# A second down product in two more gated chunks as seven smaller products, in the last chunk's order

## The chip, the cores and the metric

The kernel runs on one core of a Trainium2 chip. The metric is the device time of one execution in microseconds (us); lower is better. Three runs of the kernel before took 1439.04, 1439.17 and 1439.54 us.

## The reference

Four layers work on x, 2048 rows of 1024 numbers: linear attention (A), a gated block (B), A and B again with the same weights. Only B's down product changes here.

```python
def _B_ref(x, W_gate, W_up, W_down):        # D = 1024, F = 3584
    gate = jnp.einsum("bsd,df->bsf", x, W_gate)
    up = jnp.einsum("bsd,df->bsf", x, W_up)
    gate = gate * (gate > 0)
    h = gate * up
    return jnp.einsum("bsf,fd->bsd", h, W_down)
...
x = x + _A_ref(_layernorm(x), A_wqkv, A_wo)
x = x + _B_ref(_layernorm(x), B_W_gate, B_W_up, B_W_down)
x = x + _A_ref(_layernorm(x), A_wqkv, A_wo)
x = x + _B_ref(_layernorm(x), B_W_gate, B_W_up, B_W_down)
```

## The kernel before

A gated layer (l is 1 or 3) is done in two chunks (c is 0 or 1) of 1024 rows. In each chunk the loop over `u` makes the hidden values h in 14 units of 256 columns (`glu`), and then `down` multiplies h by W_down and adds the result to x. In layer 3 the added rows are the output: `onto` writes them to a tile `xo` (line 1437), which a DMA sends out (line 1438).

Every large product is done by a scheme for two by two blocks that needs seven block products where the plain rule needs eight. In `down` these are called 11, 21, T1, T2, 22, T3 and T4: 11, 21 and 22 use blocks of W_down as they are, the T products use sums of blocks that were made once, in layer 1, and kept in DRAM (`td`). The left side is made of blocks of h (`raw`) or of their sums e1 and e2. A result block is two by two such block results: `first` and `second` are the two groups of 512 rows, and 0 and 1 the two halves of the 1024 columns. 11 goes to first 0 and, as a start (`seed`, a ScalarE copy), to the banks Y that T2, T3 and, where T4 is not divided, T4 add to.

There are two ways to do one of the seven. `product` does it plainly: two halves of the weights (896 KB each), four banks of 128 rows by 512 columns, 56 matmuls (line 1417). `deep` divides it once more by the same scheme: seven products of 14 matmuls with 256 columns each, 98 matmuls (line 1470). For that the weights' block is prepared beforehand: `make_dd` loads it into two slots (`load_dd`), VectorE forms four sums (`sums_dd`, line 1051), and seven blocks go to DRAM (`dd`, stores at line 1042). `deep` then loads them as four entries, three of 896 KB and one of 448 KB (`load_deep`, line 1023). The left side is divided by `inner`, 16 additions of blocks on VectorE (line 1444), spread over the products that come before; within `deep`, ScalarE makes two copies (line 1479), VectorE one sum of banks (line 1495) and the additions to x (line 1430, or 1437 for output).

Before the change, T1 and 22 are divided in every chunk, T4 in all but the first, and 21 in the last chunk alone. The last chunk has an order of its own (the branch at line 1569): 11, T2, T1, T3, 21, 22, T4. The others run 11, 21, T1, T2, 22, T3, T4.

What sets the order of work around it:

- The weights come through a ring of five entries in the order of a list (`plan_B`). When an entry's use begins, `free_before` asks for the loads of the four that follow it in the list (line 1023 or 996 in `down`, lines 1172 and 1176 for the gate and up weights of a unit). The loads are issued by SP, in the order of its queue.
- All large tiles, among them the ring's entries, h (seven), e1 and e2 (two each), the two of `load_dd`, and the next chunk's normalized rows and their sums (`sums_x`, lines 1246 to 1249), share 16 slots. A tile waits until a slot is free.
- `later.at(n, f)` puts a piece of work n ticks later; `product` ticks eight times, `deep` seven times, a unit of `glu` about fourteen. So layer norms of the rows that come next, the preparation of blocks and transfers are spread over the products.
- From this program order a planner sets each engine's queue, and it lets work that is ready go ahead of work that waits.

At the head of layer 1's second chunk (units 0 to 2) VectorE also takes early row statistics for the next layer (`ln_early`), and blocks of the attention weights are loaded, summed and stored (`wq`, `tq`).

Of the kernel before, what the change touches and what calls it, by code (L numbers as in the profile page):

```python
# [92 lines left out]
class _Net:  # L93
# [906 lines left out]
    DEEP = ("T1", "22", "T4", "21")  # L1000

    def is_deep(self, l, c, p):
        return p in {(1, 0): ("T1", "22"), (3, 1): self.DEEP}.get((l, c), self.DEEP[:3])

    def order_d(self, l, c):
        if (l, c) == (3, 1):
            return "11", "T2", "T1", "T3", "21", "22", "T4"
        return "11", "21", "T1", "T2", "22", "T3", "T4"

# [642 lines left out]
    def layer_B(self, l, final):  # L1652
        ring = self.ring

        def behind(it, fn):
            with self.tc.issue_after(it.ins):
                fn()

        for c in range(2):
            hT = []  # L1660
            first = l == 1 and c == 0
            wd = {}
            for u in range(self.U):
                if u % 2 == 0:
                    hT.append(self.slot(f"h{l}_{c}_{u // 2}", dtype=F16))
                ring.load_to(ring.index((l, c, "g", u)) + 5)
                if first:
                    if u + 1 < self.U:
                        for n, w in enumerate("gu"):
                            self.later.at((4 if u else 9) + 4 * n, lambda u=u, w=w: behind(  # L1670
                                self.last_put if u else self.last_z,
                                lambda: self.make_gu(ring.get((l, c, w, u + 1)), w, u + 1)))
                    if u == 3:
                        for d in (self.U - 4, self.U - 2):
                            wd[d] = self.load_d(d)
                        self.make_dd("22", 18)
                    if u in (4, 5, 6):
                        for i, n in enumerate(range(3 * (u - 4), min(3 * (u - 3), 8))):
                            self.later.at(2 + 4 * i, lambda d=self.U - 4 + n // 4 * 2, n=n % 4: behind(
                                self.last_put, lambda: self.sums_d(wd[d], d, (n,))))  # L1680
                    if u == 7:
                        self.make_dd("T1", 1)
                if not final and c == 1:
                    if u in (0, 3):
                        self.load_w("qk"[u // 3])
                    if u in (1, 2, 4, 5):
                        for n in range(2):
                            self.later.at(4 + 5 * n, lambda w="qk"[u // 4], n=2 * (u % 3 - 1) + n: behind(
                                self.last_put, lambda: self.sums_w(w, n)))
                self.plan_inner(l, c, u, hT)  # L1690
                if u % 2 == 0 and u:
                    self.later.at(7, lambda h=hT[-2]: self.behind(self.last_put, self.third_sum, (h,)))
                if (l, c, u) in ((1, 1, 6), (3, 0, 5)):
                    self.make_dd("T4" if l == 1 else "21", 1)
                if c == 0 and u == 1:
                    for n, turn in enumerate(self.turns):
                        self.later.at(1 + n, turn)
                if c == 0 and u in (1, 2):
                    self.later.at(6, lambda u=u: behind(self.last_put, self.pairs[u - 1]))
                self.glu(l, c, u, hT)  # L1700
                if c == 0 and u == 2:
                    self.pairs[2]()
                if c == 0 and u == (self.U - 1 if first else 0):
                    after = self.last_put.ins
                if c == 1 and u == 6:
                    held = self.last_put.ins
            if c == 0:
                self.ln_chunk(l, 1, 20, 3, 3, after)
            elif not final:
                self.ln_later(l + 1, 0, 24, 3, 4, held)  # L1710
                self.ln_later(l + 1, 1, 36, 3, 4, held)
            for n in range(2 if (l, c) in ((1, 1), (3, 0)) else 0):
                self.later.at(2 + n, lambda t=n + (c == 0) * self.NS: self.bring_back(t))
            self.down(l, c, hT, final)
# [58 lines left out]
```

## Time and profile before

| | |
|---|---|
| runs, median (lowest to highest) | 1439.17 us (1439.04 to 1439.54) |
| profiled execution, first to last instruction | 1437.3 us; its own time beyond that is not listed |
| TensorE matmuls | 1429.1 us busy, 7706 |
| VectorE | 1035.7 us busy, 1991 instructions |
| ScalarE | 622.2 us busy, 1137 instructions |
| GpSimd | 309.0 us busy, 220 instructions |
| DMA | 331.31 MB, mean 231 GB/s |
| `down` of layer 1, second chunk | 648.0 to 728.7 us |
| `down` of layer 3, first chunk | 1108.2 to 1188.8 us |
| `down` of layer 3, last chunk | 1354.2 us to the end |

Times are counted from the first instruction. Engines are named PE (TensorE matmuls), PEld (TensorE weight loads), DVE (VectorE), ACT (ScalarE), POOL (GpSimd) and SP (the queue that issues most DMAs); L1470 is line 1470 of the kernel. In a row `out<-in` are the tiles written and read, xcount is the number of instructions, then come the busy time, the mean duration of one in ns, and the engine's idle time before them with what ended it. A matmul's duration includes the filling of the array, so the distance from one to the next is shorter than its duration.

### The profile page before, as it was taken

Reading aid. Unit: us, or ns where it says so; the run is one execution under the profiler, and the core shown is the slowest. Engines: PE = TensorE matmul, PEld = TensorE weight load, DVE = VectorE, ACT = ScalarE, POOL = GpSimd, SP = SyncE. Lnnn points to the kernel's source line nnn. Section 1 sums busy time; section 2 is a strip of 40 time slices with the busy share of each in tenths; the row PEclk is TensorE's granted clock in tenths of the full one; section 3 lists DMA queues with packets and bytes.
Section 4 is the critical chain, followed back from the end, with each engine's and each line's share of the span. In section 5 each row is a group of like instructions: output and inputs, shape, how many; then the busy total and the mean of one; then the engine's idle time right before and its main releaser. Section 6 shows DMA issues by size and latency. Waiting matters only on the chain.

```text
span 1437.3 us, 21281 instructions
## 1 busy us (share of the span) xinstructions
PE 1429.1 (99%) x7706; PEld 735.6 (51%) x7706; DVE 1035.7 (72%) x1991; ACT 622.2 (43%) x1137; POOL 309.0 (21%) x220
## 2 busy tenths in 40 slices
PE   9999999999999999999999999999999999999998
PEld 4444444444456444545654444445554565555457
DVE  7978698778685676558778885865766764666785
ACT  7873564233425234332058725733443434444201
POOL 1453860010100010110031577410111011111102
PEclk9999999999999999999999999999999999999999
DMA  9950787999659999866983118998878799775565
GB/s 284 243 162 8 171 208 201 292 317 292 204 190 308 350 355 334 278 216 209 292 281 100 60 22 248 278 281 261 263 226 297 225 305 281 215 203 170 175 238 180
DMA packets 360889, 331.31 MB, mean 231 GB/s; under 512 B 109840, under 2 KB 321296, under 8 KB 359760
## 3 DMA queue, kind: packets, MB, share of 16 engines
q1 hardware_dynamic: 352208, 307.15, 71.7%
q10 hardware_dynamic: 7136, 18.88, 3.5%
q0 software_dynamic: 1440, 3.93, 0.8%
q8 instruction: 60, 0.98, 0.3%
q14 instruction: 45, 0.37, 0.1%
HBM read 243.66 MB, written 61.60 MB: 212 GB/s over the span
## 4 chain that ended last, share of the span: by engine, by line
PE 94%; DVE 4%; ACT 1%; issue 0%; DMA 0%; DVEq 0%; ACTq 0%
PE ps L506 11%; PE yu L1275 9%; PE yg L1275 9%; PE dy L1417 8%; PE xg L1275 7%; PE xu L1275 6%; PE dx L1417 6%; PE i L1128 5%; PE ps L789 4%; PE zu L1275 3%; PE zg L1275 3%; PE my L588 3%; PE dyT L1470 2%; PE mv L588 2%; PE mx L588 2%; PE vu L1275 2%
## 5 line engine op out<-in xcount | busy, mean ns | idle before, releaser
L1275 PEld LDWEIGHTS <-w 128*128 128x128 f16 (+1 forms) x2768 | 270.6, 98 | 295.0 <-issue 3.7
L506 PE MATMUL ps<-w,xnT 128*128 128x512 bf16 x768 | 169.9, 379 | 0.7 <-DVE xnT L356 0.3
L1355 POOL TENSOR_TENSOR h<-m5u,m5g 128x512 f16<-128x512 f32 x28 | 37.1, 1326 | 423.4 <-DVE m5u L1351 253.4
L506 PEld LDWEIGHTS <-xnT 128*128 128x128 bf16 x768 | 74.3, 98 | 90.5 <-issue 1.8
L1275 PE MATMUL xg<-xnT,w 128*128 128x512 f16 x448 | 115.3, 379 | 0.0
L1275 PE MATMUL xu<-xnT,w 128*128 128x512 f16 x448 | 115.0, 379 | 0.0
L1417 PEld LDWEIGHTS <-h 128*128 128x128 f16 x672 | 65.7, 98 | 78.3
L1470 PEld LDWEIGHTS <-h 128*128 128x128 f16 x966 | 94.5, 98 | 12.3
L1355 POOL TENSOR_TENSOR h<-c22u,c22g 128x512 f16<-128x512 f32 x28 | 35.6, 1271 | 289.9 <-DVE c22u L1351 247.6
L1275 PE MATMUL yu<-s,w 128*128 128x512 f16 x376 | 96.5, 379 | 0.5 <-DVE zu L1331 0.5
L1275 PE MATMUL yg<-s,w 128*128 128x512 f16 x376 | 96.8, 379 | 0.0
L449 ACT ACTIVATE e<-e,eps 128x512 f32<-128x512 f32 x128 | 91.0, 720 | 3.2
L736 POOL TENSOR_TENSOR kvc<-pq,kvc 128x1024 f32<-128x1024 bf16 x32 | 78.6, 2455 | 53.1 <-DVE den L741 32.7
L1417 PE MATMUL dx<-w,h 128*128 128x512 bf16 x392 | 85.3, 379 | 0.0
L789 PE MATMUL ps<-T,pqT 128*128 128x512 bf16 x384 | 83.6, 379 | 0.0
L1302 DVE TENSOR_TENSOR h<-yu,r 128x512 f16<-128x512 f32 x56 | 38.6, 690 | 55.8 <-PE yu L1275 55.8
L1299 ACT ACTIVATE r<-yg 128x512 f32<-128x512 f32 x56 | 33.4, 597 | 101.5 <-PE yg L1275 101.5
L527 POOL TENSOR_TENSOR kvc<-kvc,slab 128x512 f32<-128x512 f32 x46 | 57.2, 1248 | 76.0 <-DVE slab L452 72.7
L448 ACT ACTIVATE e<-ps 128x512 f32<-128x512 f32 x92 | 54.2, 589 | 28.6 <-PE ps L506 28.1
L1128 PEld LDWEIGHTS <-x 128*128 128x128 f16 x504 | 49.2, 98 | 33.5 <-issue 1.9
L1299 ACT ACTIVATE r<-zg 128x512 f32<-128x512 f32 x56 | 32.8, 586 | 70.8 <-PE zg L1275 70.8
L748 POOL TENSOR_TENSOR pq<-pq,den 128x1024 bf16<-128x1024 bf16 x32 | 61.2, 1914 | 6.8 <-DVE den L743 6.8
(274 smaller groups left out, 2597.0 us busy)
## 6 DMA issues: line engine op xcount, KB each, us to landing
w<-in_B_W_gate_dram SPq DMA_DIRECT2D x56, 512.0 KB, 6.1
w<-in_B_W_up_dram SPq DMA_DIRECT2D x56, 512.0 KB, 5.4
w<-ddT SPq DMA_DIRECT2D x21, 896.0 KB, 6.3
w<-td SPq DMA_DIRECT2D x18, 896.0 KB, 4.8
x<-away SPq DMA_DIRECT2D x30, 512.0 KB, 7.5
w<-dd SPq DMA_DIRECT2D x15, 896.0 KB, 5.9
w<-in_B_W_down_dram SPq DMA_DIRECT2D x14, 896.0 KB, 6.1
away<-x SPq DMA_DIRECT2D x24, 512.0 KB, 6.8
```

What stands on the lines that cost most here:

```text
L449: self.last_exp = nc.scalar.activation(out=e, in_=e, func=ACT.Exp, scale=-1.0, bias=self.eps6[:, 0:1])
L506: nc.tensor.matmul(by_row(ps), lhsT=self.xnT[l, l_q][:, kt, j * P:(j + 1) * P], rhs=w[:, kt, :].rearrange("p (b i d) -> p i b d", i=R, d=H ...
L588: nc.tensor.matmul(banks[j], lhsT=A(i)[:, j * P:(j + 1) * P], rhs=B(i), start=start and i == 0, stop=i == NS - 1, skip_group_check=True)
L736: nc.gpsimd.tensor_tensor(out=prod, in0=pq_of[sc, j], in1=zrow, op=ALU.mult)
L748: nc.gpsimd.tensor_tensor(out=heads(pq), in0=heads(pq), in1=den[:, :].unsqueeze(2).to_broadcast([P, D // HD, HD]), op=ALU.mult)
L789: nc.tensor.matmul(ps, lhsT=pqT[sc][:, g, j * P:(j + 1) * P], rhs=T[g // 4][:, g % 4, n2 * NW:(n2 + 1) * NW], start=(g == 0), stop=(g == G ...
L1128: nc.tensor.matmul(b[:, w, :], lhsT=B[p][:, w, k, :], rhs=A[p][:, k, :], start=start and w == 0 and k == 0, stop=k == 1, skip_group_check= ...
L1275: nc.tensor.matmul(ps, lhsT=W[w][m][:, k, :], rhs=A[m][:, k, :], start=start and k == 0, stop=k == 3, skip_group_check=True)
L1299: self.last_relu = nc.scalar.activation(out=out, in_=ps, func=ACT.Relu)
L1355: nc.gpsimd.tensor_tensor(out=h[:, 3, :], in0=V["u"], in1=V["g"], op=ALU.mult)
L1417: nc.tensor.matmul(banks[j], lhsT=A(k)[:, j * P:(j + 1) * P], rhs=w[:, i, :], start=start and k == 0, stop=k == self.U - 1, skip_group_che ...
L1470: nc.tensor.matmul(out, lhsT=A[i // 2][:, i % 2, j * P:(j + 1) * P], rhs=B[m][:, i, :], start=start and i == 0 and j == 0, stop=i == NK - ...
```

## The change

Product 21 is divided in layer 1's second chunk and layer 3's first as well, and both take the last chunk's order of products. The prepared blocks of 21 are therefore needed earlier: `make_dd("21")` moves from unit 5 of layer 3's first chunk to unit 0 of layer 1's second. Layer 1's first chunk stays as it is.

```diff
     def is_deep(self, l, c, p):
-        return p in {(1, 0): ("T1", "22"), (3, 1): self.DEEP}.get((l, c), self.DEEP[:3])
+        return p in (("T1", "22") if (l, c) == (1, 0) else self.DEEP)
 
     def order_d(self, l, c):
-        if (l, c) == (3, 1):
+        if self.is_deep(l, c, "21"):
             return "11", "T2", "T1", "T3", "21", "22", "T4"
         return "11", "21", "T1", "T2", "22", "T3", "T4"
...
-                if (l, c, u) in ((1, 1, 6), (3, 0, 5)):
-                    self.make_dd("T4" if l == 1 else "21", 1)
+                if (l, c, u) in ((1, 1, 0), (1, 1, 6)):
+                    self.make_dd("T4" if u else "21", 1)
```

In `down` the branch at line 1569 asks `is_deep(l, c, "21")`, so it now serves three chunks; in it 11 is also added to x by itself (`eleven_done`, four more additions), and 21 is added by five additions from its banks instead of four.

## The prediction

> **What bounds the kernel now.** I read the page's busy times and chain first, then the waits of TensorE alone between 420 and 1430 us, which hold both chunks that change.
>
> ```profile
> span 1437.3 us, 21281 instructions
> PE 1429.1 (99%) x7706; PEld 735.6 (51%) x7706; DVE 1035.7 (72%) x1991; ACT 622.2 (43%) x1137; POOL 309.0 (21%) x220
> PE 94%; DVE 4%; ACT 1%; issue 0%; DMA 0%; DVEq 0%; ACTq 0%
> ```
>
> ```profile
> PE qx L690 <- DVE qy L681: 0.3, 1, 0.3
> PE ps L506 <- DVE pq L452: 0.2, 1, 0.2
> PE qv L690 <- DVE qm L681: 0.2, 1, 0.2
> PE fold L772 <- DVE kvc L640: 0.2, 1, 0.2
> ```
>
> The reader is to see that TensorE carries 94% of the chain and that the listed waits in 1010 us add up to 0.9 us, with no DMA among them. So the time falls by what TensorE no longer has to do, and by hardly anything else; but every wait that the change creates is paid in full.
>
> The third view is the chain in order of time (start, us, engine, tile, line, count).
>
> ```profile
> 648.00 24.17 PE dx L1417 x112
> 672.17 1.53 PE dxT L1470 x14
> 683.39 11.87 PE dy L1417 x55
> ...
> 1132.37 1.53 PE dxT L1470 x14
> 1143.41 11.87 PE dy L1417 x55
> ...
> 1366.31 12.09 PE dy L1417 x56
> 1401.31 1.53 PE dx L1470 x14
> 1412.01 1.53 PE dx L1470 x14
> ```
>
> The first five rows are the two chunks that change, layer 1's second and layer 3's first: 112 large matmuls are products 11 and 21, then come T1's small ones from 672.17 and 1132.37, then T2. The last three are the last chunk: T2 as 56 large matmuls, then the starts of the divided 21 and 22.
>
> **The change part by part.** *Matmuls.* A plain product is 56 matmuls in 12.09 us (the 1366.31 row). The divided 21 runs from 1401.31 to 1412.01, 10.70 us for 98 matmuls of half the columns. That replaces 12.09 us once in each of two chunks: 2 x 1.39 = 2.78 us saved, all of it on the path. Reordering the other six products changes no count.
>
> *Work on VectorE and ScalarE in the two down stages.*
>
> ```profile
> L1430 DVE TENSOR_TENSOR x<-x,dx 128x512 f32<-128x512 f32 x4 | 2.6, 676 | 0.0
> L1444 DVE TENSOR_TENSOR h<-e 128x512 f16<-128x512 f16 x6 | 2.3, 415 | 0.0
> L1479 ACT ACTIVATE dy<-dx 128x512 f32<-128x512 f32 x2 | 1.2, 582 | 29.5 <-PE dx L1470 29.5
> ```
>
> Product 11 now adds its four banks to x, product 21 adds five instead of four: 5 adds x 0.676 us more. The division brings 16 block sums, four of them on half-size blocks (at most 16 x 0.415 = 6.6 us), and one bank sum of an addition's size (0.7 us): at most 3.4 + 6.6 + 0.7 = 10.7 us of VectorE per chunk. ScalarE gets two copies, 1.2 us.
>
> ```profile
> 672.20:683.20 11.00, 10.85 (x99) 9.49 (x98) 11.00 (x24) 6.97 (x14) 0.00 (x0) 1.00 0.84 262
> 683.20:695.10 11.90, 11.90 (x58) 5.41 (x57) 9.01 (x17) 0.00 (x0) 0.00 (x0) 1.00 1.07 295
> 695.10:705.90 10.80, 10.80 (x99) 9.58 (x98) 8.28 (x21) 1.18 (x2) 0.00 (x0) 1.00 1.07 357
> 717.90:728.60 10.70, 10.70 (x100) 9.59 (x99) 5.36 (x9) 1.18 (x2) 0.00 (x0) 1.00 1.02 330
> 1143.20:1177.90 34.70, 34.70 (x211) 20.47 (x210) 22.20 (x55) 17.05 (x33) 4.29 (x7) 1.00 1.08 293
> 1401.20:1422.60 21.40, 21.40 (x198) 19.18 (x197) 14.87 (x35) 2.36 (x4) 5.42 (x9) 1.00 0.78 266
> ```
>
> The columns are the stretch, its length, then busy us and counts of PE, PEld, DVE, ACT and POOL, the granted clock, the DMA share and GB/s. In layer 1's second chunk VectorE is full during T1 (11.00 of 11.00), and T1 there lasts from 672.17 to 683.39, 11.22 us, against 11.04 between the matching rows at 1132.37 and 1143.41. Row statistics of the next layer sit there now, because product 21 completes half of the rows early; in the new order those halves are complete only after 21, so I expect them to move to the last product, where VectorE has 5.3 us free (5.36 of 10.70). Bounds of this step: a gain of 0.18 us, if T1 loses its delay, and a loss of 10.7 us less the idle VectorE time behind T1 (2.9 + 2.5 + 5.3 = 10.7 us in the three rows), that is none on the sum, though an addition that queues behind a block sum is late by up to its 0.4 us. I take 0.1 us of net gain, nearer the first, because the work that leaves T1 is seen and the queueing is not.
>
> *The matrix preparation moved from layer 3's chunk to layer 1's.* Preparing 21 is a read of 1792 KB, four sums and seven stores. SP issues 3 + 7 DMAs earlier, at the head of layer 1's second chunk, ahead of the gate and up loads of its third unit.
>
> ```profile
> w<-in_B_W_down_dram SPq DMA_DIRECT2D x14, 896.0 KB, 6.1
> dd<-dd SPq DMA_DIRECT2D x7, 448.0 KB, 6.4
> L1051 DVE TENSOR_TENSOR dd<-dd x4: 1079/1080/1083, 295.1 to 1042.4; 128x1792 f16<-128x1792 bf16 x4
> 495.00:505.00 10.00, 10.00 (x48) 4.49 (x47) 8.95 (x19) 3.34 (x6) 1.27 (x1) 1.00 1.10 355
> 515.00:525.00 10.00, 10.00 (x48) 4.58 (x47) 5.17 (x13) 4.14 (x8) 0.35 (x1) 1.00 1.03 348
> 479.00:551.00 72.00, 72.00 (x333) 32.36 (x331) 51.84 (x104) 28.05 (x51) 6.68 (x6) 1.00 1.06 349
> 998.00:1056.00 58.00, 58.00 (x338) 32.93 (x337) 41.27 (x61) 24.17 (x43) 6.36 (x5) 1.00 0.89 267
> ```
>
> Two halves of 896 KB are read, seven blocks of 448 KB written: 4928 KB, 5.05 MB. At the old place (998 to 1056) DMA ran at 267 GB/s and TensorE lost nothing, so leaving there gains nothing. The new place runs at 349 GB/s with a DMA share of 1.06, so 5.05 MB take 14.5 us there that no idle DMA time covers. The cover is the lead of the loads:
>
> ```profile
> 487.65 2.86 SPq L1176 DMA_DIRECT2D w<-tu  x1
> 499.00 0.59 PE L1275 MATMUL vu<-s,w 128*128 128x512 f16 x2
> 519.24 2.39 SPq L1176 DMA_DIRECT2D w<-tu  x1
> 541.71 1.03 PE L1275 MATMUL vu<-s,w 128*128 128x512 f16 x4
> w<-tu SPq DMA_DIRECT2D x6, 512.0 KB, 8.6
> ```
>
> The third unit's sums are issued at 487.65, land 8.6 us later by the median at 496.3, and are used at 499.00: 2.7 us of lead. The sixth unit's, issued at 519.24, land at 527.8 and are used at 541.71: 13.9 us. The read alone (1.835 MB at 350 GB/s = 5.2 us) in front of the third unit would cost 5.2 - 2.7 = 2.5 us, if TensorE kept this order; but only two of that product's four matmuls stand so early, and the work behind them can go first, so I take 0. The full 14.5 us against 13.9 us costs 0.6 us at the sixth unit, before any idle DMA time is made up. Bounds: 0 and 2.5 us, and I take 0.2 us, nearest the 0.6 row with part of it made up. The four sums are 4.3 us on a VectorE that is 8.95 of 10 us busy at 495 and 5.17 of 10 at 515; they can wait until there, at no cost.
>
> *More bytes in the down stages.* A divided matrix is loaded as three entries of 896 KB and one of 448, 3.21 MB instead of 1.84, and now 21, 22 and T4 follow each other. In the last chunk that runs at 266 GB/s, share 0.78, without a wait. In layer 3's first chunk the stretch from T1's end to T4's start moves 293 x 34.7 = 10.2 MB; the new one moves 1.4 MB more in 33.5 us, 346 GB/s, against 357 seen in the 695.10 row. Each entry is requested about one divided product (10.7 us) ahead.
>
> ```profile
> DMA to landing us min/median/max: 4.2/8.0/11.7
> ```
>
> That row is the divided products' loads (line 1023) between 1143 and 1190. The median leaves 2.7 us, the worst would be 1.0 us late. Bounds 0 and, with one such miss in each of the six divided products behind T3, 6 us; I take 0, nearest the median. The second sum blocks of e stay in use until 22 ends, so the slots of the next chunk's row sums come free 10.7 us before the end of layer 3's first chunk instead of earlier; 16 sums of about 0.4 us still fit beside T4.
>
> *Sum.* -2.78 - 0.1 + 0.2 = -2.7 us on the profiled execution: its span goes from 1437.3 to 1434.6 us. The median of the runs, 1439.17, is 1.9 us above that span, time around the first and last instruction that I leave as it is: 1436.5 us.
>
> *A rule that speaks against it.* The rows show 216 ns per large matmul (12.09 / 56) and 109 ns per small one (1.53 / 14). The Trainium skill, page "TensorE: Matmul & The Clock Gate", section "Back-to-back issue gap", puts a sustained stream of weight loads and matmuls at about 131 ns for 512 columns and 81 ns for 128. An estimate between these gives 98 ns for 256 columns; by it a divided product would take 9.6 us against 7.3 us plain, and the two chunks would lose 4.6 us, 1443.8 us. The trace does not agree with its 131 ns; by the rows the division pays.
>
> **The rivals.** *Late entries in the three divided products.* If each chunk misses once or twice by the worst row, 1.0 us each, plus a start of the next chunk late by as much, 2 to 3 us of the gain go: about 1439 by this worst row, and less if one chunk alone misses. For it speaks 346 GB/s wanted of 357; against it the median landing and the last chunk's freedom from waits.
>
> *Slower: the load queue of layer 1's second chunk falls behind.* SP works in order, and a store behind an unfinished transfer holds the loads behind it.
>
> ```profile
> SPq L1172 <- DMA dd<-dd: 5.2, 2, 3.4
> SPq L1042 <- DMA dd<-in_B_W_down_dram: 3.3, 1, 3.3
> ```
>
> At the old place these waits were 8.5 us together, hidden. Added to 14.5 us they make 23.0 us against 13.9 of lead: 9.1 us of waiting TensorE, 1439.2 - 2.8 + 9.1 = 1445.5 us. It decides for slower once the delay is over 13.9 + 2.8 = 16.7 us. Against it: the lead is 2.7 us only at one unit, and idle DMA time after 575 (the page's GB/s row falls there) makes some up.
>
> *Weight loads that no longer hide.* A weight load is 98 ns beside 109 ns; were it serial, 98 x 0.207 = 20.3 us per product, 8.2 us lost in each chunk: 1455.6 us. The 1401.31 and 1412.01 rows show it hidden: 98 matmuls in 10.70 us.
>
> ```profile
> L1470 PEld LDWEIGHTS <-h 128*128 128x128 f16 x308 | 30.1, 98 | 3.7
> ```
>
> **How the numbers follow.** Forecast as summed, 1436.0 to 1437.3: 0.58. A little more than the sum, under 1436.0: 0.07. Late entries, 1437.3 to 1439.5: 0.19. The queue falling behind, from about there to 1445.5: 0.15. Unhidden weight loads and the skill's spacing together: 0.01. What a measurement of this kernel can tell from no change is 0.2%, 2.9 us, nearly the whole of the saving; so even the full gain is mostly "same". Faster than 1436.3 takes the under-1436.0 case and about a quarter of the forecast: 0.24. Slower than 1442.0 takes 0.09 of the queue case, and the last: 0.10. The rest, 0.66, is within. The range 1435.9 to 1440.2 leaves out about 0.05 below and 0.13 above; the forecast's own range is 1436.0 to 1437.3.
>
> **What would show it.** Right: product 21 in both chunks as seven rows of 1.53 us in the chain, order 11, T2, T1, T3, 21, 22, T4; no PE wait on a load between 479 and 600 us; T1 at about 11.04 us in layer 1. Wrong: TensorE idle behind line 1172 or 1176 loads there, or behind line 1023 loads in 21, 22 or T4, or behind the row sums (line 1246) at the start of the last chunk.

## The result and the profile after

The changed kernel takes 1458.13 us (median of 4 runs, 1456.93 to 1459.67) beside 1439.36 us for the kernel before on the same chip: a ratio of 1.0131, 95% interval 1.0117 to 1.0146, so 18.8 us slower. The profiled execution took 1457.68 us, its span is 1455.8 us.

The head of the page of the changed kernel, busy times and chain:

```profile
span 1455.8 us, 21497 instructions
PE 1432.5 (98%) x7790; PEld 745.3 (51%) x7790; DVE 1057.1 (73%) x2035; ACT 625.6 (43%) x1141; POOL 309.4 (21%) x220
PE 90%; DVE 3%; DMA 3%; ACT 2%; SPq 1%; issue 1%; ACTq 0%; DVEq 0%
```

TensorE lost 4 points of the chain, and DMA, 0% before, and SP's queue, not listed before, now hold 4. The 84 further matmuls are two divided products (98 for 56).

From here on a *stage* runs from its first matmul to the first matmul of the next stage, read off the timeline of TensorE. Layer and chunk are given as (layer, chunk); "gated" is the gate and up part of a chunk. Stage times are those of the one profiled execution of each kernel.

| stage | before, us | after, us | difference |
|---|---|---|---|
| (1,1) gated | 168.73 | 183.44 | +14.71 |
| (1,1) down | 80.75 | 79.81 | -0.94 |
| layer 2 with (3,0) gated | 379.45 | 380.72 | +1.27 |
| (3,0) down | 80.57 | 84.06 | +3.49 |
| (3,1) gated | 165.46 | 165.53 | +0.07 |
| all others | | | -0.1 |

These add up to the 18.5 us between the spans. TensorE's waits in the changed kernel between 420 and 1452 us (what, on what; us, times, longest):

```profile
PE vu L1275 <- DMA w<-tu: 8.4, 1, 8.4
PE dyT L1470 <- DMA w<-ddT: 3.1, 1, 3.1
PE i L1128 <- DMA x<-gi: 1.4, 1, 1.4
PE qx L690 <- DVE x L452: 0.9, 1, 0.9
```

The waits before added up to 0.9 us without a DMA; these four are new, and the first three are for loads (`tu`: sums of up weights; `ddT`: prepared blocks of T4; `gi`: blocks that were put to DRAM earlier and come back). The longest stands at the third unit of (1,1). SP's timeline there (start, us, line, count) and what it waited for between 479 and 520 us:

```profile
486.08 6.60 SPq L1034 DMA_DIRECT2D dd<-in_B_W_down_dram  x3
496.68 0.37 SPq L1042 DMA_DIRECT2D dd<-dd  x1
497.15 0.50 SPq L1172 DMA_DIRECT2D w<-in_B_W_up_dram  x1
499.25 0.97 SPq L1042 DMA_DIRECT2D dd<-dd  x2
500.27 1.88 SPq L1176 DMA_DIRECT2D w<-tu  x1
...
SPq L1042 <- DMA dd<-in_B_W_down_dram: 5.4, 2, 3.9
```

The preparation's loads went out at 486.08, its first store had to wait for them, and the third unit's sums (`w<-tu`) were issued at 500.27 instead of 487.65, 12.6 us later. TensorE's timeline and then its stretches (busy us and counts of PE, PEld, DVE, ACT, POOL; granted clock, DMA share, GB/s):

```profile
498.17 1.03 PE L1275 MATMUL yu<-s,w 128*128 128x512 f16 x4
507.62 1.46 PE L1275 MATMUL vu<-s,w 128*128 128x512 f16 x3 [8.43 <-DMA w<-tu]
508.88 1.91 PE L1275 MATMUL yg<-s,w 128*128 128x512 f16 x4
...
485.00:495.00 10.00, 10.00 (x48) 4.53 (x47) 7.84 (x17) 3.67 (x7) 1.27 (x1) 1.00 1.08 359
495.00:505.00 10.00, 4.19 (x19) 1.64 (x17) 9.45 (x16) 1.56 (x5) 0.00 (x0) 0.81 0.96 289
505.00:515.00 10.00, 7.38 (x26) 3.01 (x27) 2.95 (x5) 1.11 (x2) 1.18 (x1) 0.67 1.05 354
```

TensorE resumes at 507.62, and the four `yg` matmuls behind the wait take 1.91 us, where the four `yu` ahead of it took 1.03, at a granted clock of 0.67: the wait costs a second time, 1.9 us in the nine matmuls behind it (427 ns from one to the next instead of 216). With the wait itself, 8.6 us from matmul to matmul, that is 10.5 us. The rest of the 14.7 us, 4.2 us, are shorter stalls between 580 and 607 us, on `x<-gi` and on ScalarE's and VectorE's work for it.

The other large loss is in (3,0)'s down stage, in T4, on TensorE's timeline:

```profile
1193.10 1.69 PE L1470 MATMUL dzT<-w,h 128*128 128x256 f16 x14
1197.86 3.17 PE L1470 MATMUL dyT<-w,h 128*128 128x256 f16 x14 [3.08 <-DMA w<-ddT]
1200.82 1.80 PE L1470 MATMUL dxT<-w,h 128*128 128x256 f16 x14
...
1191.60 1.50 SPq L1023 DMA_DIRECT2D w<-ddT  x3
```

The last row is SP's: T4's second entry was issued at 1191.60, 3.0 us before TensorE came to it, and landed 6.2 us later. TensorE waits (3.24 us counted from matmul to matmul), the 14 matmuls behind it again run at half speed (3.17 us, against 1.69 us of the group ahead, 1.5 to 1.6 us more), and the divided product saves 1.39: 3.24 + 1.6 - 1.39 = 3.45 of the 3.49 us measured.

### The profile page after: what moved, and what is told of

Same layout as the page of the kernel before. It is cut to its first block, busy times and chain, and to the rows that moved or that the text cites. A ratio compares the mean times of both kernels' runs of the same rounds, so it can differ in the third digit from the quotient of the medians.

```text
span 1455.8 us, 21497 instructions
## 1 busy us (share of the span) xinstructions
PE 1432.5 (98%) x7790; PEld 745.3 (51%) x7790; DVE 1057.1 (73%) x2035; ACT 625.6 (43%) x1141; POOL 309.4 (21%) x220
## 4 chain that ended last, share of the span: by engine, by line
PE 90%; DVE 3%; DMA 3%; ACT 2%; SPq 1%; issue 1%; ACTq 0%; DVEq 0%
PE ps L506 11%; PE yg L1275 8%; PE yu L1275 8%; PE dy L1417 7%; PE xg L1275 6%; PE xu L1275 6%; PE i L1128 5%; PE dx L1417 4%; PE ps L789 4%; PE zg L1275 3%; PE zu L1275 3%; PE my L588 3%; PE dyT L1470 2%; PE dy L1470 2%; PE mv L588 2%; PE mx L588 2%
## 5 line engine op out<-in xcount | busy, mean ns | idle before, releaser
L1417 PE MATMUL dy<-w,h 128*128 128x512 f16 x280 | 61.6, 379 | 0.0
```

What stands on the lines that cost most here:

```text
L1417: nc.tensor.matmul(banks[j], lhsT=A(k)[:, j * P:(j + 1) * P], rhs=w[:, i, :], start=start and k == 0, stop=k == self.U - 1, skip_group_che ...
```

## The experiments

Three theories were put against one another for the gated stage: **order** (SP stands before the preparation's stores, with the third unit's load behind them), **bytes** (DMA is full from 480 to 600 us, and 5.05 MB more push back whatever is behind them, in any order) and **buffers** (two of the sixteen big buffers are held). I began with *order*, which the rows above seem to show.

### The preparation alone, and the division alone

Preparation moved, products as before (on the kernel before):

```
-                if (l, c, u) in ((1, 1, 6), (3, 0, 5)):
-                    self.make_dd("T4" if l == 1 else "21", 1)
+                if (l, c, u) in ((1, 1, 0), (1, 1, 6)):
+                    self.make_dd("T4" if u else "21", 1)
```

> Layer 1's second chunk and layer 3's first chunk keep their plain 21 and the old order of products; only the preparation of the 21 weights is moved, from the sixth unit of layer 3's first chunk to the first unit of layer 1's second chunk. If the place of the preparation alone makes the loss there (its stores stand in SP's queue behind its own unfinished loads, and the third unit's up weights are issued 12.6 us later), the gated stage of layer 1's second chunk is again about 14.7 us longer (183.4 instead of 168.7 us between the down stages) with the 8 us idle time before the third unit's up product, and the time is 1453 to 1455 us. If the loss comes from the divided products and their order, that stage stays at 168.7 us and the time is 1438 to 1440 us.

Measured: 1456.0 us (ratio 1.0111, 1.0094 to 1.0128), 1 us over the expected range, and the gated stage takes 183.89 us. The place of the preparation makes the whole of that stage's loss; the divided products have no part in it.

(3,0) alone divided, preparation at its old place:

```
-        return p in {(1, 0): ("T1", "22"), (3, 1): self.DEEP}.get((l, c), self.DEEP[:3])
+        return p in {(1, 0): ("T1", "22"), (1, 1): self.DEEP[:3]}.get((l, c), self.DEEP)
...
-        if (l, c) == (3, 1):
+        if self.is_deep(l, c, "21"):
```

> Only layer 3's first chunk gets the divided 21 and the new order; the preparation stays in that chunk's own gated stage (sixth unit), and layer 1's second chunk is as before. If the down stage of layer 3's first chunk loses its 3.5 us by itself (T4's entry is asked for too late because its buffer is held to the end of 22), this stage takes 83 to 84 us instead of 80.6 and the time is 1441 to 1444 us. If the loss there only follows from the delay upstream, the stage gets shorter by the 1.4 us of the divided product, to 79.2 us, and the time is 1437.5 to 1438.5 us.

Measured: 1442.23 us (1.0022, 1.0012 to 1.0031). The down stage takes 81.22 us, under the 83 to 84 expected, but the next gated stage takes 167.61 instead of 165.46: with 2.8 us lost in the two, the loss is (3,0)'s own and not brought on from upstream. TensorE's waits there:

```profile
PE vu L1275 <- DMA w<-tu: 2.0, 1, 2.0
PE dyT L1470 <- DMA w<-ddT: 1.6, 1, 1.6
```

### Order, bytes or buffers in the gated stage

The preparation 14 ticks later in the same unit, behind the third unit's loads (on the changed kernel):

```
-                    self.make_dd("T4" if u else "21", 1)
+                    self.make_dd("T4" if u else "21", 1 if u else 15)
```

> The changed kernel, with the preparation of the 21 weights begun 14 ticks later in the same first unit, so that SP issues the third unit's up weights ahead of it; the bytes and the stage are the same. If the order on SP is the cause, the idle time of 8 us before the third unit's up product and the slow clock behind it go, the gated stage is at 170 to 174 us instead of 183.4, and the time is 1446 to 1449 us. If there are too many bytes for the stage, the wait comes back at the next unit or the one after, the stage stays at 180 us or more and the time at 1455 us or more.

Measured: 1459.13 us (1.0139, 1.0118 to 1.016), gated stage 183.54 us. The wait before `vu` is gone, and about as much, 14.8 us, is lost further on; TensorE's waits from 479 to 665 us begin:

```profile
PE i L1128 <- DMA x<-gi: 5.0, 2, 3.3
PE yu L1275 <- DVE m5u L1351: 2.1, 1, 2.1
PE yg L1275 <- DVE zg L1331: 1.0, 1, 1.0
```

That went against *order* as I had put it: the order decides where the loss shows, not how large it is.

Both preparations later, at the seventh and the tenth unit (on the changed kernel):

```
-                if (l, c, u) in ((1, 1, 0), (1, 1, 6)):
-                    self.make_dd("T4" if u else "21", 1)
+                if (l, c, u) in ((1, 1, 6), (1, 1, 9)):
+                    self.make_dd("21" if u == 6 else "T4", 1)
```

> The changed kernel, with both preparations later in the gated stage of layer 1's second chunk: that of the 21 weights at the seventh unit, where that of T4 was, and that of T4 at the tenth. By the theory of SP's order the stage loses most of its 14.7 us, since TensorE has more lead in the later units: 169 to 171 us, and the time is 1443 to 1446 us, what is left being the down stage of layer 3's first chunk. By the rival that any further 9 MB (loads and stores together, as counted in the prediction's windows) in this stage costs their transfer time, wherever they stand, the stage stays above 178 us and the time above 1452 us.

Measured: 1444.07 us (1.0034, 1.0023 to 1.0046), gated stage 169.20 us. (The 9 MB of that text is a slip: one preparation is 5.05 MB, the two are 10.1 MB, and only 5.05 are new to the stage.) Two stretches of the kernel before, then the same two of this one:

```profile
480.00:550.00 70.00, 70.00 (x323) 31.47 (x322) 50.40 (x102) 28.05 (x51) 6.34 (x5) 1.00 1.06 349
600.00:648.00 48.00, 48.00 (x243) 23.64 (x242) 24.63 (x43) 18.33 (x32) 6.35 (x5) 1.00 0.64 210
```

```profile
480.00:550.00 70.00, 70.00 (x324) 31.34 (x322) 50.49 (x102) 28.05 (x51) 6.35 (x5) 1.00 1.06 355
600.00:648.00 48.00, 47.73 (x242) 23.35 (x240) 28.58 (x47) 18.15 (x32) 6.35 (x5) 1.00 0.94 309
```

From 600 to 648 us the rate goes from 210 to 309 GB/s: 99 GB/s x 48 us = 4.75 MB, about one preparation (T4's, which now stands there while 21's has its old place), in idle DMA time; the stage is 0.5 us longer. This agrees with both theories: later there is more lead, and there is DMA time to spare.

The loads of the preparation alone, without sums and stores (on the kernel before, into two buffers nobody reads):

```
+                if (l, c, u) == (1, 1, 0):
+                    self.later.at(1, self.load_only)
...
+    def load_only(self):
+        half = self.U // 2
+        for i in range(2):
+            t = self.slot(f"lo{i}", [P, half, NW])
+            src = self.src_d("21", slice(i * half, (i + 1) * half))
+            self.nc.sync.dma_start(out=t[:, :, :].bitcast(src.dtype), in_=src)
```

> The kernel before, with the two loads of the 21 weights alone (1.835 MB) at the first unit of layer 1's second chunk, into two buffers that nothing reads: no sums and no stores there, and everything else as before. If the loss is the transfer time of the added bytes in a stretch in which the DMA engines are full, this dose costs 1.835 MB at 350 GB/s = 5.2 us, a little less or more by rate: stage 173 to 175 us, time 1443 to 1446 us. If the loss comes from SP standing before the stores (which are gone here), it costs under 1 us: 1439 to 1440 us.

Measured: 1445.18 us (1.004, 1.0026 to 1.0054), gated stage 173.73 us, 5.0 us longer: the 1.835 MB cost about what they take to move (5.2 us), with no store for SP to stand before. The runs of this kernel lie between 1442.57 and 1447.54 us, so the nearness of the two numbers is that of one execution. TensorE's one wait there:

```profile
PE vu L1282 <- DMA w<-tu: 3.1, 1, 3.1
```

The wait is 3.2 us from matmul to matmul; the rest is 1.7 us of slow clock behind it.

Bytes alone, first try: six copies from DRAM to DRAM on the POOL queue (on the kernel before):

```
+                if (l, c, u) == (1, 1, 0):
+                    for n in range(6):
+                        self.later.at(1 + 3 * n, lambda n=n: self.copy(n, 1 + n // 5))
```

> The kernel before, with nothing but six copies from DRAM to DRAM added on the POOL queue in the first two units of layer 1's second chunk: 5.05 MB, as many as the preparation moves, without a buffer, without an instruction on SP and without a reader. If it is the bytes in a full stretch, whoever issues them, the stage is 12 to 16 us longer (181 to 185 us instead of 168.7) and the time is 1451 to 1455 us. If SP's order or its buffers make the loss, the stage gets no more than 3 us longer: below 1443 us.

Measured: 1443.24 us (1.0028, 1.0018 to 1.0039), gated stage 168.73 us. It says nothing on the question: the copies depended on nothing and ran between 57 and 103 us, where they delayed layer 0. The second try reads rows that are stored to DRAM only at the end of (1,0)'s down stage:

```
+                if (l, c, u) == (1, 1, 0):
+                    for n in range(10):
+                        self.later.at(1 + n, lambda n=n: self.copy(n))
...
+        self.nc.gpsimd.dma_start(out=self.spare[n], in_=self.away[4 + n % 4])
```

> The kernel before, with ten copies from DRAM to DRAM on the POOL queue, 5.24 MB, that read what the end of layer 1's first down stage has stored (its stores land at 485 to 488 us), so that they run from about 487 us on: the preparation's bytes without its buffers and without an instruction on SP. If the bytes make the loss, the stage gets 11 to 16 us longer (180 to 185 us instead of 168.7): 1450 to 1455 us. If it is SP's order or the buffers, it gets at most 3 us longer: 1439 to 1442.5 us.

Measured: 1455.96 us (1.0113, 1.0098 to 1.0128), gated stage 186.00 us, a little over the range. TensorE's only wait from 479 to 665 us, two rows of SP's timeline, and the DMA issues from 485 to 515 us (count, KB, median us to landing):

```profile
PE vu L1279 <- DMA w<-tu: 15.6, 1, 15.6
...
483.77 18.03 SPq L1220 DMA_DIRECT2D wq<-in_A_wqkv_dram  x2
503.49 5.06 SPq L1180 DMA_DIRECT2D w<-tu  x1
...
spare<-away POOLq DMA_DIRECT2D x10, 512.0 KB, 9.7
wq<-in_A_wqkv_dram SPq DMA_DIRECT2D x2, 512.0 KB, 25.1
```

SP has no new instruction, and yet its `w<-tu` goes out at 503.49 instead of 487.65: the two `wq` loads ahead of it take 25.1 us to land, and SP is held in issuing them from 483.77 to 501.80. Of the 10.26 MB moved from 485 to 515 us, 5.24 were the copies. At the 349 GB/s of the stretch these take 15.0 us; the stage lost 17.3, of which 1.6 are slow clock.

Buffers alone: two big buffers held for 30 ticks, no transfer (on the kernel before):

```
+    def hold(self):
+        t = [self.slot(f"ho{i}") for i in range(2)]
+        for x in t:
+            self.nc.vector.memset(x[:, 0, 0:8], 0.0)
+        for i, x in enumerate(t):
+            self.later.at(30, lambda x=x: self.behind(self.last_put, lambda x: self.nc.vector.memset(x[:, 0, 0:8], 0.0), (x,)))
```

> The kernel before, with two of the big buffers taken at the first unit of layer 1's second chunk and held for 30 ticks (into the third unit) with a few bytes set in them, no transfer at all. If the missing buffers make the loss (loads asked for later), the stage gets more than 5 us longer: above 1444 us. If bytes or SP's order make it, the stage stays within 1 us: 1439 to 1440.5 us.

Measured: 1439.15 us (1.0001, 0.9992 to 1.0011), gated stage 168.75 us. The two were held for 18.5 us (487.6 to 506.1) and cost nothing. The changed kernel holds its two longer, from 486 us until behind its last store at 518 us, so this run alone does not clear them; but the copies hold none and make the loss all the same.

The stores on POOL's queue (on the changed kernel):

```
-            self.nc.sync.dma_start(out=self.dd[p][:, m, :, :], in_=b.bitcast(F16))
+            queue = self.nc.gpsimd if p == "21" else self.nc.sync
+            queue.dma_start(out=self.dd[p][:, m, :, :], in_=b.bitcast(F16))
```

> The changed kernel, with the seven stores of the 21 preparation on the POOL queue instead of SP's; the same loads, bytes and buffers. If SP standing before the stores makes the loss, the 8.4 us wait before the third unit's up product shrinks to that of the loads alone (3.2 us in the run with loads only) and the stage is at 172 to 176 us instead of 183.4: 1446 to 1450 us. If the bytes make it, the stage stays above 180 us and the time above 1454 us.

Measured: 1456.1 us (1.0118, 1.0098 to 1.0137), gated stage 181.97 us. The wait before `vu` shrinks by half, and sums of VectorE that come late take its place:

```profile
PE vu L1276 <- DMA w<-tu: 4.7, 1, 4.7
PE yg L1276 <- DVE zg L1332: 3.7, 3, 1.6
```

So the loss of the gated stage comes from the bytes in a stretch whose DMA is full and is about their transfer time, and SP's standing before its stores only chooses the instruction that pays first. That 14.7 us lies so near the 14.5 us of transfer is partly chance: 1.9 us of it are slow clock, and the waits and stalls themselves are 12.8 us, somewhat less than the transfer, as the 2.7 us of lead would have one expect. The runs of these kernels also differ among themselves (1455.68 to 1463.31 us with the later preparation).

### What the division itself brings in layer 1's second chunk

The preparation from the last unit of (1,0) on, so that its bytes go into (1,0)'s down stage; only (1,1) newly divided (on the changed kernel):

```
-        return p in (("T1", "22") if (l, c) == (1, 0) else self.DEEP)
+        return p in {(1, 0): ("T1", "22"), (3, 0): self.DEEP[:3]}.get((l, c), self.DEEP)
...
-                if (l, c, u) in ((1, 1, 0), (1, 1, 6)):
-                    self.make_dd("T4" if u else "21", 1)
+                if (l, c, u) in ((1, 0, 13), (1, 1, 6)):
+                    self.make_dd("T4" if c else "21", 1)
```

> 21 divided in layer 1's second chunk with the new order, layer 3's first chunk as before; the 21 weights are prepared from the last unit of layer 1's first chunk on, so that their bytes fall mostly into that chunk's down stage, and T4's preparation stands where it was. If the bytes in the full stretch are the cause, the gated stage behind is at 168.5 to 170 us, the down stage of layer 1's second chunk at 79.4 to 80.6 us, and the time is 1437.5 to 1440 us. If the divided products and their order cost something of their own in that chunk, the time is above 1441 us.

Measured: 1439.7 us (1.0005, 0.9996 to 1.0014). The gated stage is at 168.73 us, to the hundredth that of before, and (1,0)'s down stage at 81.96, also unchanged: in this execution the 5.05 MB are free. They are not far from costing something: the third unit's sums go out 1.7 us later in the stage than before, which its 2.7 us of lead still cover. The down stage gains 0.95 us, and the stage behind it loses 1.27. TensorE's waits from 640 to 770 us:

```profile
PE qx L690 <- DVE x L452: 0.9, 1, 0.9
PE dy L1470 <- DVE x L1430: 0.2, 1, 0.2
```

The first twenty us of that stage, before and with the early preparation:

```profile
728.60:738.60 10.00, 10.00 (x49) 4.58 (x47) 10.00 (x25) 6.77 (x12) 4.50 (x3) 1.00 1.04 402
738.60:748.60 10.00, 10.00 (x48) 4.52 (x47) 8.38 (x14) 7.88 (x15) 5.79 (x6) 1.00 0.92 248
```

```profile
727.90:737.90 10.00, 10.00 (x49) 4.56 (x48) 9.80 (x20) 6.70 (x12) 1.82 (x2) 1.00 1.09 369
737.90:747.90 10.00, 9.02 (x42) 3.96 (x41) 9.04 (x18) 6.81 (x13) 6.70 (x6) 1.00 1.06 349
```

VectorE is nearly full in both, and in the new order it has 0.66 us more left for the second ten, where TensorE now waits for it.

The same with 22 ahead of 21 in (1,1):

```
+            if (l, c) != (3, 1):
+                return "11", "T2", "T1", "T3", "22", "21", "T4"
...
+                deep("22", parts, put_into(first, 1))
...
+                deep("21", parts2, put_into(first, 0))
+                deep("T4", parts, put_into(second, 0))
```

> The kernel with the early preparation (1439.7 us), where only layer 1's second chunk gets the divided 21, with 22 ahead of 21 there. With 21 first, the down stage gained 0.95 us and layer 2's attention lost 1.27; with 22 first these were 0.69 and 0.38 us in the earlier run. If both carry over, the time is 0.6 us below the early version's, 1438.5 to 1439.5 us, and equals the kernel before within the bound; if the attention stage loses its 1.27 us here too, 1439.5 to 1440.5 us.

Measured: 1439.51 us (1.0002, 0.9993 to 1.0011). Down stage 80.07, the stage behind it 379.86: together 0.27 us under before, as hoped, but 1.2 us are lost at the third unit of the gated stage (169.94), where `w<-tu`, issued 3.4 us later in the stage than before, is late, and 0.3 in (1,0)'s down stage (82.25). The preparation stands where it stood in the run above, so that place is not free in every execution. No version found here is faster than the kernel before.

### The down stage of layer 3's first chunk

Delay moves here between the down stage and the gated stage behind it, so the two are added: 246.03 us before, 249.59 changed, 249.42 with late preparations. The first four runs stand on that last kernel (1444.07 us), the others on the kernel before.

22 ahead of 21 in both chunks, edit as above:

> The kernel with both preparations late in layer 1's second chunk (1444.1 us, down stages of 80.6 us in layer 1's second chunk and 84.0 in layer 3's first), with 22 ahead of 21 in the two newly divided chunks, so that the buffer e2 comes free one product earlier and T4's entries can be asked for about 10 us earlier. If the late release of that buffer is what makes T4 wait 3.0 us in layer 3's first chunk, the wait goes and the time is 1440 to 1441.5 us. If what makes it wait is that the DMA engines are full from 1140 to 1210 us (share 1.0 to 1.17) and get 1.4 MB more to carry, about 4.3 us at 320 GB/s, the wait only moves to another product or to the next stage, and the time stays at 1443 to 1445 us.

Measured: 1446.77 us (1.0053, 1.0037 to 1.0069), the two stages 253.29 us. TensorE waits 5.9 us for VectorE, which from 1176 to 1195 us stands before a sum over transposed rows:

```profile
PE dyT L1472 <- DVE dzT L1497: 5.9, 1, 5.9
...
DVE s L1248 <- DMA xnT<-xnb: 7.0, 1, 7.0
```

T4's first entries did come in time, as an early release of e2 would have it; a late transpose took their place. With those sums four ticks later:

```
-            self.later.at(39 + 3 * j, lambda j=j: self.behind(
+            self.later.at((39 if (l, c) != (3, 1) else 43) + 3 * j, lambda j=j: self.behind(
```

> The run with 22 ahead of 21 (1446.8 us, layer 3's first down stage 87.8 us, with 5.9 us in which T4 waits for VectorE's sum of z, which stands behind the sums over transposed rows), with these sums four ticks (about 6 us) later in layer 3's second chunk's preparation. If VectorE's order alone makes that wait, it goes for the most part and T4's entries are in time, as they were there: stage 80 to 82 us, time 1440 to 1442.5 us. If T4's entries come late again, or the transposed rows are late for the next stage as well, the stage and its neighbour stay 3 us or more behind: 1443 us or more.

Measured: 1442.77 us (1.0022, 1.0013 to 1.0031). The down stage is at 80.23 us, so VectorE's order made that wait; and the next gated stage is at 169.87, so the two are at 250.10. TensorE's waits are the next unit's loads:

```profile
PE xu L1277 <- DMA w<-in_B_W_up_dram: 2.7, 1, 2.7
PE dyT L1472 <- DMA w<-ddT: 0.6, 1, 0.6
```

The transposes issued by ScalarE:

```
-        nc.sync.dma_start_transpose(out=self.xnT[layer, q][:, :, j * P:(j + 1) * P], in_=xn)
+        queue = nc.scalar if (layer, q // 2) == (3, 1) else nc.sync
+        queue.dma_start_transpose(out=self.xnT[layer, q][:, :, j * P:(j + 1) * P], in_=xn)
```

> The kernel with both preparations late (1444.1 us), with the eight transposes of layer 3's second chunk issued by ScalarE instead of SP, so that SP no longer stands behind them (15 us of its waits from 1140 to 1190 us are for ScalarE's rows ahead of a transpose). If SP's order is what asks for T4's entries too late in layer 3's first chunk, its 3.0 us wait goes and this down stage is at 80 to 81 us instead of 84.0: 1440.5 to 1442 us. If the DMA engines are full and the bytes decide, the stage and its neighbour lose as much as before: 1443 to 1445 us.

Measured: 1446.02 us (four runs, 1445.25 to 1455.07; 1.0069, 1.0043 to 1.0096), the two stages 251.31 us. TensorE's waits:

```profile
PE dy L1471 <- DVE xo L1438: 2.2, 1, 2.2
PE vu L1276 <- DMA w<-tu: 1.5, 1, 1.5
PE dy L1471 <- DVE dz L1496: 1.1, 2, 0.7
PE dyT L1471 <- DMA w<-ddT: 0.7, 1, 0.7
```

T4's own wait falls to 0.7 us, but 3.3 us for VectorE and 1.5 for the next unit's load come instead. Taking the transposes out of SP's order does not shorten the stage; it moves the wait.

The output stores of (3,0) left out:

```
-                queue.dma_start(out=self.o_v[:, ts.start + s.start:ts.start + s.stop, cols], in_=xo[:, s, :])
+                if c == 1:
+                    queue.dma_start(out=self.o_v[:, ts.start + s.start:ts.start + s.stop, cols], in_=xo[:, s, :])
```

> The kernel with both preparations late (1444.1 us), with the stores of layer 3's first chunk to the output left out (2.1 MB on the POOL queue, from 1150 to 1200 us); the sums are still made. If the bytes of that stretch are the cause of the loss in layer 3's first chunk (84.0 us instead of 80.6), it goes: the stage is at 79.5 to 81 us and the time is 1439.5 to 1441 us. If SP's order or the buffers are the cause, T4's wait stays above 2 us and the time at 1443 us or more.

Measured: 1441.14 us (1.0014, 1.0004 to 1.0023), the two stages 247.23 us: 2.2 of the 3.4 us come back, between the two expectations.

Bytes alone on the kernel before, first try:

```
+            if (l, c) == (3, 0):
+                for n in range(2):
+                    self.later.at(22 + 4 * n, lambda n=n: self.copy(n, 1 + n))
```

> The kernel before, with two copies from DRAM to DRAM added on the POOL queue in the down stage of layer 3's first chunk: 1.376 MB, as many bytes as the divided 21 adds there. If the bytes make the loss (about 4.5 us beyond the saved product), this costs 3 to 5 us in that stage and the unit behind it: 1442 to 1444.5 us. If buffers or SP's order make it, the copies are free: 1439 to 1440 us.

Measured: 1439.67 us (1.0003, 0.9994 to 1.0012), but these copies ran at 58 and 84 us, so the run tells nothing of this stage. The second try stores twelve output pieces twice:

```
+                if c == 0 and (cols.start or ts.start >= QT):
+                    queue.dma_start(out=self.spare[:, ts.start + s.start:ts.start + s.stop, cols], in_=xo[:, s, :])
```

> The kernel before, with twelve of the sixteen output stores of layer 3's first chunk done a second time into a spare place (1.57 MB on the POOL queue, from about 1150 to 1195 us), a little more than the 1.38 MB that the divided 21 adds there. If bytes alone make the loss of that stage, this costs 3 to 6 us in it and the unit behind it: 1442 to 1445 us. If the shorter lead of the entries (four buffers for one product instead of two) is needed for a loss, it costs under 1 us: 1439 to 1440 us.

Measured: 1440.44 us (1.0009, 0.9999 to 1.0018), down stage 80.57 us as before, the two 246.43 us. 1.57 MB cost 0.4 us there, though DMA was full there too (a share of 1.08 in the prediction's row 1143.20:1177.90). Another 0.9 us of this execution lie in (1,1)'s gated stage, where nothing was changed: so much a stage can differ from one execution to the next.

Two buffers held for 14 ticks from T2's end, with no transfer:

```
+            if (l, c) == (3, 0):
+                self.later.at(31, self.hold)
```

> The kernel before, with two of the big buffers held for 14 ticks (about 20 us) from the end of T2 on in the down stage of layer 3's first chunk, with no transfer: about what the new order does to e2, which it holds until 22 is done. If the missing buffers make T4's late entries, T4 waits here too and the stage and its neighbour lose 2 us or more: 1441 us or more. If it takes the divided products with their bytes as well, less than 1 us: 1439 to 1440 us.

Measured: 1440.2 us (1.0009, 0.9999 to 1.0018), the two stages 247.33 us, between the two expectations. TensorE's waits there:

```profile
PE vu L1281 <- DMA w<-tu: 0.7, 1, 0.7
PE dyT L1476 <- DVE dzT L1501: 0.3, 1, 0.3
```

So of the 3.4 us that the two stages lose, 4.8 with the saved product, 0.4 follow bytes alone and 1.3 missing buffers alone. Neither alone makes the loss, and each change of order moved the wait to another transfer. Bytes and buffers together, without the new order, were not tried, so what makes the rest stays open.

## Why the prediction was wrong, point by point

- **Matmuls, -2.78 us: right in kind.** 98 matmuls replace 56 twice. In (1,1) 0.94 of 1.39 us arrived: T1 gained 0.18 us, the upper bound (0.1 was taken), and two stalls of 0.2 and 0.4 us came in the divided 21. The profile puts the longer one down to VectorE in the early-preparation run and to a load in the changed kernel.
- **VectorE, "none on the sum": wrong by 1.27 us.** I looked at VectorE's room in the down stage alone. The sixteen row statistics run in a denser block, 708.2 to 732.1 us in the early-preparation run (668.4 to 741.9 before), seven of them behind the stage's end in both kernels; VectorE is then late by a microsecond in layer 2's attention, which I had not looked at. Which of its instructions makes it late was not tried.
- **The moved preparation, +0.2 us: the step that failed; it cost 14.7.** The text had both numbers that make the answer: 14.5 us of transfer "that no idle DMA time covers", and 2.7 us of lead at the third unit. I then set the 14.5 us against the sixth unit's 13.9 us, and waved the third unit off because "the work behind them can go first". It did not: `vu` stands as early as before (behind `yu` at 498.17 in the changed kernel), and TensorE waits with everything behind it. Beyond that, a lead pays only once: the delayed queue stays delayed until DMA has idle time (from 600 us on in the kernel before, at 210 GB/s; not after 575 us, as the text has it), and every later load with little lead collects the rest, so the loss is about the transfer time wherever in this stretch the preparation starts (183.89, 183.54 and 181.97 us by three orders). The bound of 2.5 us for the loads alone came near the wait (3.1 us by the profile) and left out the slow clock behind it.
- **More bytes in the down stages, 0 us: wrong by 4.8 us in (3,0).** "Each entry is requested about one divided product ahead" took the lead from the last chunk's pace. T4's second entry took 6.2 us to land, inside the quoted landing times, but it was asked for only 3.0 us ahead.
- **The rivals.** *The load queue falls behind* was the one that came, at 1458 instead of 1445.5 us: its place is right, its price is not (9.1 us against 14.7, from the 13.9 us of lead again), and its mechanism only in part. It adds SP's waits before stores to the bytes; the run with bytes alone shows that these waits are not needed. *Late entries* came true in (3,0) at 3.5 us instead of 1 to 2. *Weight loads that no longer hide* did not come: 98 matmuls still take about 10.7 us where nothing waits. (The chance for faster than 1436.3, 0.24, is a little above its own parts: 0.07 and a quarter of 0.58 make 0.22.)

## What to carry to other kernels

In (1,1)'s gated stage, where DMA and TensorE were both full, a moved transfer cost about its transfer time, whatever queue issued it and in whatever order, until the first stretch with idle DMA time; so look for that stretch (here 210 GB/s from 600 us on, or the last unit of the chunk before) and put the bytes there. Full DMA engines alone do not set this price: in (3,0)'s down stage 1.57 MB, 4.5 us at 350 GB/s, cost 0.4 us. So the leads of the loads behind must count as well; no run varied them alone. Compare a delay with the smallest lead behind it, not with a convenient one, and take it that TensorE keeps its order. To tell bytes, buffers and queue order apart, add each alone; and tie an added transfer to data that exist only at that time, or it runs hundreds of microseconds early.

## What the runs showed of the hardware

**A wait of TensorE above some 2.9 us is paid for twice.** Idle times of 1.9, 2.1, 2.2, 2.4 and 2.7 us were followed by full speed; those of 2.9, 3.0, 3.2 (two), 3.8, 6.1, 8.6, 8.9 and 15.7 us by 3.0 to 4.6 us at half speed (427 ns a large matmul, 213 a small one), at a cost of 1.5 to 2.3 us, whatever the length of the wait. (They are counted from matmul to matmul, about 0.2 us more than the profile lists: its 2.7 us before `xu` are the 2.9 here.) After 3.4 us (the later preparation) and 4.8 us (stores on POOL's queue), where short waits kept interrupting, the slow clock cost 2.6 and 3.3 us. The Trainium skill, page "TensorE: Matmul & The Clock Gate", section "What's actually happening", gives a cause: the array falls to half clock after an idle window of about 3.4 us and comes back after about 3.4 us of work, and the window runs freely. The traces agree with the length of the slow stretch; the shortest idle time that set it off here was 2.9 us, less than a full window, which the rule as it stands does not give.

**Over 70 us the rate hardly moved with the demand.** From 480 to 550 us DMA moved 349 GB/s before, 342 with the preparation moved, 334 in the changed kernel and 354 with 5.24 MB of copies on a second queue; with the copies, SP's own loads of `wq` took 25.1 us to land instead of 9.0, and SP was held in issuing them (18.03 us for two loads). The Trainium skill, page "DMA: Bandwidth & Descriptors", section "Specifications", gives about 358 GB/s as one core's limit on HBM. The four rates lie under it, but these runs do not show that it is what holds them: single stretches of 10 us showed up to 417, and a copy, which reads and writes DRAM, is counted once (336.56 MB in that run, 331.31 before). What sets the rate stays open.
